# Attention, two feed-forward layers: output stores moved in the last stage, its last block taken product by product, and another order of the opening

## The chip, the core and the metric

The kernel runs on one core of one Trainium2 chip. The metric is the device time of one execution, in microseconds (us). The engines are named as in the profile: PE (TensorE; PEld is its weight load), DVE (VectorE), ACT (ScalarE), POOL (GpSimd) and SP (SyncE, which here issues the DMAs).

## The reference

Three layers follow each other on 3072 tokens of 512 values (4 batches of 768, 8 heads of 64).

- Attention in chunks of 32 queries: each chunk sees 16 keys ahead of it, its own 32, 8 behind it, and 8 memory keys; softmax of the scaled scores, times the values.
- A feed-forward layer with SoLU: `h = x @ w_in` (512 to 1024), `solu = h * softmax(h)`, a layer norm over the 1024 with the gain `g_ln`, and `@ w_out` (1024 to 512).
- A feed-forward layer with hard swish: `h = x @ w_in` (512 to 2048), `g = h * clip(h + 3, 0, 6) / 6`, and `@ w_out` (2048 to 512).

```python
    h = x @ w_in
    e = np.exp(h - np.max(h, axis=-1, keepdims=True))
    solu = h * e / (np.sum(e, axis=-1, keepdims=True) + 1e-09)
    ln = (solu - mu) / np.sqrt(var + 1e-06) * g_ln
    x = ln @ w_out
    ...
    h = x @ w2_in
    out = (h * np.clip(h + 3.0, 0.0, 6.0) / 6.0) @ w2_out
```

The four weight matrices come as 64-bit floats; the other inputs and the output are 32-bit.

## The kernel before

The order of all work is written out by hand. A list of names is run through from the left; each name issues the instructions of one step on the engines that it uses. Each engine takes its own instructions in the order of the list, so the list is the order of every engine and of SP's queue of DMAs at once. What a step has to wait for is worked out from the tiles that it reads and writes.

**Products in two parts.** A 32-bit operand is split into a high part (rounded, by a copy on ACT) and a low part (the rest, by a subtraction, mostly on DVE). Each product is then three matmuls: high by high, high by low, low by high.

**The opening.** `FIRST` is a list of some 530 entries. It brings the kernel from nothing to its steady loop, which starts with token tile 7 (a tile has 128 tokens). Its entries:

- `load_q`, `load_k`, `load_v`, `load_mem_k`: loads of a tile's q, k, v, and of the memory keys, all on SP. `load_v` has ten DMAs for tiles 0 and 1 (two of them `mem_v`), eight for most others; `load_k` has two. Two tiles share a buffer in turn, so the load of tile i waits for the last reader of tile i - 2. `zero` clears a buffer once.
- `q_p`, `k_p` (two parts a tile), `mem_p`: transposes on PE, `q_e`, `k_e`, `mem_e` their copies out of PSUM (L298 on ACT, L300 on DVE or POOL). `s_p`: scores on PE (L522). `s_max`, `s_sub`, `s_exp`, `s_sum`, `s_norm`: the softmax, on DVE but for `s_exp` (ACT) and `s_norm` where the entry names POOL. `p_p`, `p_e`: the probabilities transposed and copied. `v_p`: times the values (L578). `x_h`, `x_l`: the result split.
- `load_w1:u`, u = 0 to 7: a quarter of one half of `w_in`, 512 KB, 64-bit. `w1_abs`, `w1_hold`, `w1_bits` (three steps), `w1_hi`, `w1_lo` turn it into a 32-bit high and low part. `load_wo`, `wo_abs`, ..., `wo_lo` do the same for the first `w_out`, `load_w2`, `w2_abs`, ..., `w2_store` for the second layer's weights.
- `m1:i,f,half`: the first product of tile i (L609). Unit u of `w_in` is f = u // 4 and kt = u % 4; `half` takes kt 0 and 1 or 2 and 3, six matmuls of 512 columns. `m1:0,1,0` needs units 4 and 5, `m1:0,0,0` units 0 and 1.
- `ln_...`: SoLU and layer norm of a tile; `ln_p`, `ln_h`, `ln_l` transpose and split it. `m2:0,n`: the second product of three tiles (L694).
- `warm:n`: n transposes of the identity on PE (L1043), whose results nobody reads.
- An entry's last letter is its engine: A for ACT, D for DVE, P for POOL.

**The loop.** `BODY` is run for tiles 7 to 23. Its first PE step is `m1:0`.

**The last layer** is taken block by block with a scheme of seven products (1 to 7) for each pair of 2 x 2 blocks in place of eight. Its second product runs in `G_SEQ`, 96 units (t, j): t is one of 12 blocks of 256 tokens, j one of 8 pieces of the inner dimension. `g4(i)` (L990) does unit i on PE: seven products of three matmuls with 256 columns, in `ORDER_B`, summed up over j in four PSUM banks (product 1 in bank 0; 6 and 2 in bank 1; 7 and 5 in bank 2; 4 and 3 in bank 3). For odd t, banks 0 and 1 are halves of one tile, and banks 2 and 3 are tiles of their own.

Ahead of `g4(i)`, `g_load` fetches the operand from DRAM (L963, SP), `g_sum` adds and subtracts (L969, DVE), `g_hi` (ACT) and `g_lo` (DVE, both L79x) split it. The loop at the end of the function fetches unit i + 5, prepares i + 3 and the low part of i + 2 in step i. After the last piece of a block (j = 7) its four banks become the output: `q1` (ACT, L998) copies product 1, four `q_sum` (DVE, L1001) add the rest, `q_store` (SP, L1018) issues four stores of 128 KB. Before, this stood in two steps behind the block:

```python
            if j == NU - 1:
                drains = [[("q1", t), ("q_sum", t, 1), ("q_sum", t, 2)],
                          [("q_sum", t, 3), ("q_sum", t, 4), ("q_store", t, 0), ("q_store", t, 1)]]
```

Of the kernel before, what the change touches and what calls it, by code (L numbers as in the profile page):

```python
# [30 lines left out]
    s_max:0 k_p:2,0 k_p:2,1 w1_hold:2,D s_sub:0 s_exp:0 k_e:1,1,A s_p:1 s_sum:0 load_w1:0 w1_abs:0,A w1_bits:2,0
    w1_bits:2,1 s_max:1 k_e:2,1,A load_q:2 load_mem_k:1 k_e:2,0,A w1_hi:3,P q_p:2 s_norm:0,D warm:9 p_p:0 load_w1:4
    w1_bits:2,2 load_k:3 s_sub:1 q_e:2,0,A w1_hold:0,P w1_abs:4,A load_k:4 q_e:2,1,A warm:5 k_p:3,0 w1_hold:4,D
    w1_bits:0,0 p_e:0,1,A w1_bits:0,1 s_p:2 s_exp:1 s_sum:1 mem_p:2 p_e:0,0,A s_norm:1,D w1_bits:4,0 consts load_q:3
# [11 lines left out]
    wo_hold:0,P wo_hold:1,D load_k:7 ln_max:1 s_p:5 p_e:3,1,A s_edge:5 p_e:3,0,A wo_bits:0,0 s_max:5 s_norm:4,D
    k_p:6,1 m1:2,1,0 k_e:6,1,A load_q:6 q_p:6 load_wo:2 wo_abs:2,A m1:2,0,0 wo_hold:2,P ln_sq:0 ln_var:0 ln_pow:0
    load_v:3 k_mem:6,D s_sub:5 wo_bits:1,0 q_e:6,0,A q_e:6,1,A wo_bits:2,0 wo_bits:2,1 v_p:3 ln_exp:1 p_p:4 ln_den:1
    k_p:6,0 x_h:3,1 ln_norm:0 m1:2,0,1 x_l:3,1 s_exp:5 wo_bits:1,1 ln_solu:1 p_e:4,0,A wo_bits:0,1 ln_mean:1
    wo_bits:0,2 p_e:4,1,A ln_p:0,0 wo_bits:2,2 load_wo:3 wo_abs:3,A m1:2,1,1 wo_hold:3,D wo_bits:1,2 k_e:6,0,A wo_g:0  # L50
    ln_h:0,0,1 ln_sq:1 s_p:6 wo_hi:0,A wo_g:1 ln_var:1 ln_max:2 s_sum:5 s_norm:5,D wo_hi:1,P load_q:7 wo_bits:5,0
    s_edge:6 ln_l:0,0,1 load_v:4 v_p:4 ln_p:0,1 ln_exp:2 ln_pow:1 load_wo:4 m1:3,0,0 wo_abs:4,A load_wo:6 q_p:7
    load_q:8 q_e:7,1,A x_h:4,1 ln_h:0,1,1 m1:3,1,0 load_k:8 m1:3,1,1 x_l:4,1 ln_den:2 k_p:7,1 k_e:7,1,A wo_g:2
    m1:3,0,1 wo_hi:2,A q_e:7,0,A k_p:7,0 ln_norm:1 ln_l:0,1,1 s_max:6 ln_solu:2 ln_mean:2 s_sub:6 p_p:5 ln_sq:2
    ln_p:1,0 wo_lo:0,P ln_max:3 s_exp:6 k_e:7,0,A m1:4,1,0 p_e:5,0,D wo_bits:5,1 ln_var:2 wo_bits:3,0 wo_lo:1,P
    wo_bits:3,1 ln_p:1,1 wo_bits:5,2 load_k:9 wo_abs:6,A m1:4,0,0 ln_exp:3 ln_pow:2 ln_h:1,0,1 m1:4,1,1 ln_den:3
    ln_norm:2 p_e:5,1,A wo_bits:3,2 ln_solu:3 early_close ln_p:2,0 load_v:5 m1:4,0,1 wo_hold:4,P ln_l:1,0,1 wo_g:3
    ln_max:4 load_wo:7 s_sum:6 ln_h:1,1,1 wo_bits:4,0 ln_h:2,0,1 wo_bits:4,1 ln_exp:4 s_p:7 load_q:9 ln_l:1,1,1 v_p:5
    ln_l:2,0,1 ln_mean:3 x_h:5,1 ln_sq:3 wo_hold:6,P load_v:6 ln_den:4 ln_p:2,1 ln_h:2,1,1 ln_solu:4 ln_mean:4 k_p:8,0
    m2:0,0 wo_hi:3,D q_p:8 q_e:8,1,A x_l:5,1 ln_var:3 ln_pow:3 q_e:8,0,A m2:0,3 ln_sq:4 wo_bits:6,0 wo_bits:6,1  # L60
    k_p:8,1 m1:5,0 s_norm:6,P s_max:7 k_e:8,0,D s_sub:7 wo_bits:6,2 ln_var:4 wo_g:5 s_exp:7 k_e:8,1,A p_p:6 p_e:6,1,A
    wo_bits:4,2 wo_g:4 load_v:7 wo_lo:2,P wo_lo:3,D ln_norm:3 m1:5,1 wo_hi:5,P s_sum:7 p_e:6,0,A wo_hi:4,A wo_lo:4,P
    v_p:6 s_p:8 ln_max:5 ln_exp:5 ln_p:3,1 x_h:6,1 ln_l:2,1,1 m2:0,1 ln_p:3,0 ln_h:3,0,1 ln_h:3,1,0 wo_abs:7,D wo_g:6
    load_w2:1 wo_hi:6,A wo_hold:7,D s_norm:7,P ln_den:5 m2:0,4 ln_solu:5 wo_bits:7,0 wo_bits:7,1 p_p:7 wo_bits:7,2
    p_e:7,1,A x_l:6,1 m1:6,1 m1:6,0 ln_mean:5 p_e:7,0,D wo_g:7 wo_lo:6,D load_w2:0 ln_l:3,1,0 v_p:7 wo_lo:5,D load_v:9
    wo_hi:7,P ln_sq:5 ln_var:5 ln_pow:4 w2_abs:1,A ln_norm:4 ln_pow:5 ln_p:4,1 ln_max:6 wo_lo:7,P ln_exp:6 m2:0,2
    load_k:10 m2_e:0,0 ln_p:4,0 w2_abs:0,A ln_den:6 s_max:8 w2_hold:1,D m2:0,5 w2_bits:1,0 w2_bits:1,1 w2_bits:1,2
    load_w2:3 w2_store:1 ln_l:3,0,1 m2_e:0,1 m2:0,6 m2:0,7 m2:0,9 m2_s:0,1 ln_h:4,1,0 x_h:7,0 m2:0,10 x_l:7,0
    ln_solu:6 ln_mean:6 ln_norm:5 ln_sq:6 ln_p:5,1 m2:0,11 ln_p:5,0 ln_l:4,1,0 ln_h:5,1,0 ln_h:4,0,0 w2_abs:3,A
    m2_s:0,0 ln_l:5,1,0 m2:0,8 ln_l:4,0,0 ln_var:6 ln_pow:6 w2_hold:3,P ln_norm:6 m2_e:0,3 m2_e:0,2 load_v:8 s_sub:8  # L70
# [1292 lines left out]
```

## Time and profile before

| What | Value |
|---|---|
| Time, median of 3 runs | 877.47 us (877.0 to 877.73) |
| The profiled execution, its own time | 878.19 us |
| Its span, first to last instruction | 876.4 us |
| PE busy | 859.8 us, 98% of the span |
| DVE busy | 749.3 us, 86% |
| ACT busy | 466.8 us, 53% |
| POOL busy | 263.9 us, 30% |

All times in the rows count from the start of the span. A busy PE in the table counts the whole length of each matmul, and matmuls overlap; waits are what a matmul stood idle for. The chain of work that ended last is 80% PE and 9% DVE.

### The profile page before, as it was taken

The page shows a single profiled execution, that of the slowest core. Times are in us where ns is not written, and L with a number is a line of the kernel's source. Part 1 is how long each engine was busy: PE and PEld are TensorE (multiplying, and loading weights), DVE is VectorE, ACT ScalarE, POOL GpSimd, SP SyncE. Part 2 cuts the span into 40 slices and gives each one's busy share as a digit, 9 for nine tenths or more (in the row PEclk, how much of TensorE's full clock was granted, in tenths as well). Part 3 has the DMA queues.
Part 4 walks back from the last instruction along what each step waited for, and adds up shares of the span by engine and source line. Part 5 has one row for each costly group of instructions (what it writes and reads, how often), then busy time and mean ns, then how long its engine had stood idle before and what let it go on. Part 6 is the DMA issues. An engine that isn't in the chain of part 4 may idle for free.

```text
span 876.4 us, 20127 instructions
## 1 busy us (share of the span) xinstructions
PE 859.8 (98%) x7523; PEld 811.8 (93%) x7523; DVE 749.3 (86%) x1593; ACT 466.8 (53%) x865; POOL 263.9 (30%) x233
## 2 busy tenths in 40 slices
...
PEclk9999999999999999999999999999999999999999
...
GB/s 228 190 234 132 86 127 205 255 196 266 272 273 248 234 297 224 149 169 224 249 182 135 240 143 215 185 157 228 255 261 219 169 138 138 147 124 135 136 137 74
DMA packets 184013, 168.26 MB, mean 192 GB/s; under 512 B 107116, under 2 KB 154220, under 8 KB 183916
## 3 DMA queue, kind: packets, MB, share of 16 engines
...
## 4 chain that ended last, share of the span: by engine, by line
PE 80%; DVE 9%; DMA 5%; issue 2%; ACT 2%; SPq 2%; POOL 0%; ACTq 0%; DVEq 0%; POOLq 0%
PE acc L903 25%; PE acc L990 20%; PE m L694 14%; PE h L609 12%; PE tp L666 2%; PE tp L578 2%; PE sc L522 2%; DMA q_raw<-in_q_dram 1%; DVE f_s L1001 1%; PE tp L560 1%; PE tp L509 1%; DVE f_xl L969 1%; DMA w1raw<-in_moe_w_in_dram 1%; DVE f_kn L969 1%; PE tp L494 1%
## 5 line engine op out<-in xcount | busy, mean ns | idle before, releaser
L694 PE MATMUL m<-lnh,wo 128*128 128x384 f32 x512 | 138.3, 344 | 0.0
L938 ACT ACTIVATE f_s<-f_e,constants 128x512 f32<-128x512 f32 x96 | 68.1, 720 | 76.5 <-DVE f_e L931 60.5
L609 PE MATMUL h<-w,xh 128*128 128x512 f32 x336 | 106.3, 397 | 0.1
L694 PEld LDWEIGHTS m<-lnh,wo 128*128 128x128 f32 x512 | 91.7, 189 | 0.2
L694 PE MATMUL m<-lnl,wo 128*128 128x384 f32 x256 | 88.2, 345 | 0.0
L311 POOL TENSOR_SCALAR w2t<-w2t 128x512 f32<-128x512 f32 x30 | 58.9, 1965 | 44.9 <-ACT w2t L304 44.9
L609 PEld LDWEIGHTS h<-w,xh 128*128 128x128 f32 x336 | 61.0, 188 | 11.6 <-ACT lnh L337 0.3
L941 DVE SCALAR_TENSOR_TENSOR f_s<-f_s,f_e 128x512 f32<-128x512 f32 x96 | 70.5, 742 | 0.9 <-ACT f_s L938 0.9
L609 PE MATMUL h<-w,xl 128*128 128x512 f32 x168 | 65.7, 391 | 0.0
L298 ACT ACTIVATE kT<-tp 128x448 f32<-128x448 f32 (+3 forms) x61 | 24.7, 457 | 53.6 <-PE tp L494 46.2
L694 PEld LDWEIGHTS m<-lnl,wo 128*128 128x128 f32 x256 | 48.2, 189 | 0.0
L793 ACT ACTIVATE b_qb<-f_kn 128x384 fp32r<-128x384 f32 (+1 forms) x48 | 27.4, 571 | 33.8 <-DVE f_kn L969 27.6
L624 ACT ACTIVATE e<-h,lst 128x1024 f32<-128x1024 f32 x24 | 26.5, 1103 | 24.1 <-DVE lst L618 24.0
L298 ACT ACTIVATE qb<-tp 64x512 f32<-64x512 f32 x48 | 28.5, 593 | 19.4 <-PE tp L509 18.9
L609 PEld LDWEIGHTS h<-w,xl 128*128 128x128 f32 x168 | 31.5, 188 | 6.9
L935 DVE TENSOR_TENSOR f_e<-acc,f_e 128x512 f32<-128x512 f32 x48 | 32.9, 685 | 2.1 <-PE acc L903 0.4
L793 ACT ACTIVATE b_km<-f_xl 128x512 fp32r<-128x512 f32 x26 | 16.4, 631 | 34.2 <-DVE f_xl L969 26.6
L927 DVE TENSOR_TENSOR f_e<-acc,f_e 128x512 f32<-128x512 f32 x48 | 32.8, 684 | 1.2 <-PE acc L903 0.3
L341 DVE TENSOR_TENSOR lnl<-tp,lnh 128x512 fp32r<-128x512 f32 x41 | 26.7, 686 | 7.7 <-ACT lnh L337 7.7
L618 DVE TENSOR_REDUCE lst<-h 128x1 f32<-128x1024 f32 x24 | 29.2, 1217 | 4.4 <-PE h L609 4.2
L644 ACT ACTIVATE e<-so,lst 128x1024 f32<-128x1024 f32 x24 | 27.4, 1143 | 7.6 <-DVE lst L640 7.6
L635 DVE SCALAR_TENSOR_TENSOR so<-h,lst,e 128x1024 f32<-128x1024 f32 x24 | 30.7, 1278 | 0.5
...
## 6 DMA issues: line engine op xcount, KB each, us to landing
...
```

The costliest lines, as they stand in the source:

```text
L298: ACT.activation(out=out, in_=in_, func=AF.Copy)
L311: ENG[eng].tensor_scalar(out=tf, in0=tf, scalar1=U_LO, scalar2=U_HI, op0=ALU.max, op1=ALU.min)
L609: PE.matmul(h[:, f], a[:, kt], w[kt][:, f * 512:(f + 1) * 512], start=n == 0, stop=n == 3 * NKT - 1)
L635: DVE.scalar_tensor_tensor(out=so_t[i], in0=h_t.pop(i).rearrange("p a b -> p (a b)"), scalar=st[:, 5:6], in1=e_t[i], op0=ALU.mult, op1=ALU ...
L694: PE.matmul(acc, w[fc // 2][:, fc % 2, dc * P:(dc + 1) * P], a[:, fc], start=n == 0, stop=n == len(todo) - 1)
L793: ACT.activation(out=hl[0], in_=r, func=AF.Copy)
L903: PE.matmul(o, w[wl][:, c * P:(c + 1) * P], x[xl][:, c], start=m == 0 and half == 0, stop=m == 5, skip_group_check=True)
L927: DVE.tensor_tensor(c_of(n)[1], bank(n % 2, 2), wide(c_of(n)[0][:, 1]), ALU.add)
L935: DVE.tensor_tensor(c, bank(n % 2, 3), c, ALU.add)
L938: ACT.activation(out=g_of(n)[k], in_=c_of(n)[k], func=AF.Relu, bias=three, scale=1.0)
L941: DVE.scalar_tensor_tensor(out=g_of(n)[k], in0=g_of(n)[k], scalar=6.0, in1=c_of(n)[k], op0=ALU.min, op1=ALU.mult)
L990: PE.matmul(bank(t % 2, k)[:, half], g[al][:, G_BLOCK[p]], b_op[j, p][bl], start=j == 0 and m == 0 and half == 0, stop=j == NU - 1 and m = ...
```

## The change

Three things change.

**Stores of a block.** The sums and stores behind a block stand in four steps of the loop instead of two: `q1` and the first sum; the second; the third and fourth; the stores.

**The last block.** The last two units (t = 11, j = 6 and 7) are no longer taken one after the other. Products 1, 6 and 2 of both come first, then 7 and 5 of both, then 4 of both, then 3 of both. Then come `q1` and the sums; the fourth sum is taken in two halves (`q_half`), and each of the four stores is issued behind its data, two of them by ACT.

**The opening.** `FIRST` has the same steps in another order. 61 warm transposes stand for 71. The engine of some entries changes: 19 entries that named DVE no longer do, 24 others now do; POOL loses 14 and gains 9, ACT loses and gains 14.

```diff
 FIRST = """
-    zero:v1,P load_q:0 zero:qb,P zero:pb,P load_w1:1 zero:v0,D warm:15 q_p:0 zero:km0,D load_mem_k:0 zero:kn1,D
-    zero:kn0,P w1_abs:1,D warm:12 mem_p:0 w1_hold:1,P mem_e:0,D load_w1:3 zero:km1,D w1_abs:3,D load_k:0 q_e:0,1,A
...
-    q_p:3 s_max:2 k_e:3,0,A mem_p:1 q_e:3,0,A w1_bits:0,2 mem_e:2,A q_e:3,1,A s_sub:2 load_v:0 spread_mem_v:0,0,A
-    load_q:4 warm:4 k_p:3,1 mem_e:1,D w1_lo:3,D k_e:3,1,A s_exp:2 k_p:4,1 s_p:3 load_w1:6 w1_hi:0,P
-    spread_mem_v:0,64,A warm:1 v_p:0 s_sum:2 k_e:4,1,A p_p:1 load_w1:5 w1_hi:2,A x_h:0,0 w1_bits:4,1 w1_abs:6,A
-    k_p:4,0 load_v:1 w1_lo:2,D p_e:1,1,A load_k:5 warm:1 q_p:4 p_e:1,0,A load_w1:7 x_l:0,0 w1_hold:6,D w1_bits:6,0
-    w1_abs:5,D w1_lo:0,P s_max:3 k_e:4,0,A w1_bits:4,2 load_q:5 s_norm:2,P m1:0,0,0 q_e:4,1,A s_sub:3 w1_bits:6,1
-    w1_bits:6,2 w1_hold:5,P p_p:2 load_k:6 w1_bits:5,0 spread_mem_v:1,64,A m1:0,0,1 spread_mem_v:1,0,A v_p:1 q_e:4,0,A
-    w1_hi:6,A w1_bits:5,1 s_p:4 k_p:5,1 x_h:1,0 w1_hi:4,A x_l:1,0 early_open m1:1,0,0 w1_bits:5,2 p_e:2,0,A p_e:2,1,A
-    w1_abs:7,A s_max:4 load_wo:5 w1_hi:5,A w1_hold:7,D q_p:5 w1_lo:6,P k_p:5,0 load_wo:0 q_e:5,0,A w1_lo:5,D
...
+    zero:kn0,P zero:km0,D zero:kn1,D load_w1:4 zero:km1,D zero:v0,D w1_abs:4,D w1_hold:4,D w1_bits:4,0 zero:pb,P
+    w1_bits:4,1 w1_bits:4,2 zero:v1,P load_mem_k:0 warm:20 mem_p:0 mem_e:0,A load_mem_k:3 load_k:0 load_q:0 load_w1:0
+    warm:3 k_p:0,0 w1_hi:4,D k_e:0,0,A q_p:0 zero:qb,P q_e:0,1,A k_p:0,1 mem_p:3 q_e:0,0,A k_mem:0,D mem_e:3,D
...
+    load_k:3 mem_p:1 q_e:2,0,A s_sub:1 load_q:3 k_p:2,1 k_e:2,1,A w1_bits:6,2 mem_e:1,A w1_bits:7,2 w1_bits:5,0
+    k_p:3,1 k_p:3,0 load_v:0 s_exp:1 load_k:4 w1_hi:7,A w1_bits:5,1 s_sum:1 spread_mem_v:0,64,A load_w1:1 s_p:2
+    s_norm:1,P spread_mem_v:0,0,A q_p:3 load_q:4 k_e:3,1,A warm:2 v_p:0 w1_lo:7,D k_e:3,0,A q_e:3,1,A s_max:2 k_p:4,1
+    q_e:3,0,D w1_bits:5,2 w1_hi:6,A w1_lo:6,P w1_hi:5,A w1_lo:5,P s_sub:2 x_h:0,0 x_l:0,0 load_w1:3 s_exp:2 p_p:1
+    p_e:1,0,A w1_abs:1,A p_e:1,1,A s_p:3 k_p:4,0 k_e:4,0,A k_e:4,1,A m1:0,1,0 s_sum:2 s_norm:2,D q_p:4 p_p:2 load_v:1
+    w1_hold:1,P load_w1:2 s_max:3 s_sub:3 q_e:4,1,A m1:0,1,1 w1_bits:1,0 w1_abs:3,D w1_bits:1,1 w1_bits:1,2 w1_hi:1,D
+    load_k:5 w1_lo:1,D q_e:4,0,A spread_mem_v:1,0,A s_p:4 spread_mem_v:1,64,A v_p:1 x_h:1,0 load_q:5 w1_hold:3,P
+    w1_bits:3,0 p_e:2,0,A w1_bits:3,1 consts w1_abs:2,A x_l:1,0 w1_bits:3,2 w1_hold:2,D load_v:2 load_wo:7 p_e:2,1,A
+    m1:0,0,0 w1_bits:2,0 w1_bits:2,1 early_open m1:1,0,0 w1_bits:2,2 w1_hi:3,A w1_hi:2,A w1_lo:2,P load_k:6 s_exp:3
+    w1_lo:3,D k_p:5,1 k_e:5,1,D q_p:5 q_e:5,0,A k_p:5,0 k_e:5,0,A q_e:5,1,A s_max:4 load_g s_sum:3 s_norm:3,D m1:1,1,0
...
+    wo_hold:3,D wo_g:5 ln_mean:4 ln_h:2,1,1 load_wo:6 wo_lo:0,D ln_solu:3 early_close ln_sq:4 ln_mean:3 wo_hi:1,A
+    m1:5,0 k_e:8,0,A wo_g:2 ln_sq:3 wo_hi:2,A p_p:6 m1:5,1 wo_bits:3,0 load_q:8 wo_g:4 wo_bits:3,1 wo_lo:1,D ln_var:3
+    ln_l:2,1,1 wo_bits:3,2 m2:0,0 ln_var:4 wo_hi:5,A ln_pow:3 ln_pow:4 p_e:6,0,A wo_hi:4,A wo_lo:4,P wo_g:3 p_e:6,1,A
...
-    def g4(i):
+    def g4(i, products=ORDER_B):
         t, j = G_SEQ[i]
         g = g_hl(i)
-        for p in ORDER_B:
+        for p in products:
...
+    def q_half(t, n):
+        c = out_of(t)[1][:, n]
+        sixth(c, bank(t % 2, 3)[:, n], c)
+
+    def q_put(t, k, n, eng=SP):
+        h = 1 - n if k == 0 else n
+        eng.dma_start(out=out[t * TG + n * P:t * TG + (n + 1) * P, 256 * h:256 * h + 256], in_=out_of(t)[k][:, n])
...
-            if i > 23:
+            if 23 < i < len(G_SEQ) - 2:
                 emit("g4", i)
...
             if j == NU - 1:
-                drains = [[("q1", t), ("q_sum", t, 1), ("q_sum", t, 2)],
-                          [("q_sum", t, 3), ("q_sum", t, 4), ("q_store", t, 0), ("q_store", t, 1)]]
-        for step in drains:
-            for name, *a in step:
-                emit(name, *a)
+                drains = [[("q1", t), ("q_sum", t, 1)], [("q_sum", t, 2)], [("q_sum", t, 3), ("q_sum", t, 4)],
+                          [("q_store", t, 0), ("q_store", t, 1)]]
+        for products in ((1, 6, 2), (7, 5), (4,), (3,)):
+            for i in (len(G_SEQ) - 2, len(G_SEQ) - 1):
+                g4(i, products)
+        q1(t)
+        q_sum(t, 1)
+        q_put(t, 0, 1, ACT)
+        q_sum(t, 2)
+        q_sum(t, 3)
+        q_put(t, 0, 0, ACT)
+        q_half(t, 0)
+        q_put(t, 1, 0)
+        q_half(t, 1)
+        q_put(t, 1, 1)
```

## Rows read from the trace of the kernel before

**Rows 1.** The page: span, and PE's granted clock (tenths) in 40 slices.
```profile
span 876.4 us, 20127 instructions
...
PEclk9999999999999999999999999999999999999999
```

**Rows 2.** Busy times by stretch: PE, PEld, DVE, ACT, POOL; clock, DMA share, GB/s.
```profile
48.00:92.00 44.00, 41.63 (x398) 32.91 (x396) 41.08 (x84) 34.42 (x61) 25.43 (x19) 1.00 0.68 162
...
675.00:871.00 196.00, 194.26 (x1688) 192.48 (x1687) 177.74 (x512) 86.36 (x168) 0.00 (x0) 1.00 0.42 132
```

**Rows 3.** Waits of PE from 32 to 92 us: total, times, longest (eight rows, four shown).
```profile
PE tp L509 <- DMA q_raw<-in_q_dram: 1.6, 1, 1.6
PE tp L666 <- ACT lnh L337: 1.0, 1, 1.0
...
PE tp L560 <- ACT pb L298: 0.4, 1, 0.4
...
PE tp L480 <- DMA kn<-in_k_dram: 0.2, 1, 0.2
```

**Rows 4.** Waits of PE from 675 to 871 us.
```profile
PE acc L990 <- DVE b_v L796: 0.8, 2, 0.6
PE acc L990 <- DVE b_kT L796: 0.7, 4, 0.2
```

**Rows 5.** Timeline of the tail, all engines: start, length, instructions, idle time ahead.
```profile
865.92 2.20 PE L990 MATMUL acc<-b_ll,b_v 128*128 128x256 f32 x18
...
866.60 0.68 DVE L796 TENSOR_TENSOR b_e<-f_kn,b_e 128x512 fp32r<-128x512 f32 x1
...
868.30 2.20 PE L990 MATMUL acc<-b_wo,b_e 128*128 128x256 f32 x18
869.52 0.38 ACT L998 ACTIVATE f_pe<-acc 128x256 f32<-128x256 f32 x1 [3.16 <-PE acc L990]
...
870.34 0.50 PE L990 MATMUL acc<-b_pn,b_e 128*128 128x256 f32 x3
870.73 1.95 DVE L1001 SCALAR_TENSOR_TENSOR f_s<-acc,f_s 128x512 f32<-128x512 f32 x3
871.91 1.80 SPq L1018 DMA_DIRECT2D out_dram<-f_s  x4
```

**Rows 6.** The output sums' line L1001: shortest, median and longest in ns.
```profile
L1001 DVE SCALAR_TENSOR_TENSOR f_s<-acc,f_s x36: 411/691/692, 675.0 to 872.0; 128x512 f32<-128x512 f32 x24, 128x256 f32<-128x256 f32 x12
```

**Rows 7.** Timeline of SP's queue behind a block's end, 733 to 765 us.
```profile
740.70 1.80 SPq L1018 DMA_DIRECT2D out_dram<-f_s  x4
742.61 0.53 SPq L963 DMA_DIRECT2D f_z<-g  x1
```

**Rows 8.** Waits of DVE from 675 to 872 us.
```profile
DVE f_kn L969 <- DMA f_z<-g: 8.0, 9, 2.2
```

**Rows 9.** Groups by line and form, 0 to 110 us: a low part on DVE.
```profile
L384 DVE TENSOR_TENSOR w<-w1raw,w 128x512 fp32r<-128x512 f32 x4 | 2.8, 690 | 0.3 <-ACT w L298 0.2
```

**Rows 10.** Timeline of PE in the opening.
```profile
1.34 3.46 PE L1043 MATMUL idle<-ident 128*128 128x128 f32 x15 [1.34 <-POOL ident masks.py:199]
...
5.39 1.47 PE L1043 MATMUL idle<-ident 128*128 128x128 f32 x12
...
28.74 1.17 PE L578 MATMUL tp<-pb,v 128*64 128x64 f32 x32
...
31.95 0.70 PE L609 MATMUL h<-w,xh 128*128 128x512 f32 x2
...
39.70 1.64 PE L609 MATMUL h<-w,xx 128*128 128x512 f32 x6
42.98 0.63 PE L509 MATMUL tp<-ident,q_raw 128*128 128x128 f32 x4 [1.64 <-DMA q_raw<-in_q_dram]
```

**Rows 11.** Timeline of SP's queue in the opening.
```profile
23.89 2.48 SPq L273 DMA_DIRECT2D v<-in_v_dram  x4
...
37.27 0.43 SPq L239 DMA_DIRECT2D q_raw<-in_q_dram  x1
```

More of the change, by code (lines that the diff above doesn't have):

```diff
@@ L31 @@
[L31 to L34, printed above, removed]
-    q_p:3 s_max:2 k_e:3,0,A mem_p:1 q_e:3,0,A w1_bits:0,2 mem_e:2,A q_e:3,1,A s_sub:2 load_v:0 spread_mem_v:0,0,A
@@ L46 @@
[L46 to L70, printed above, removed]
@@ new lines @@
+    s_max:0 s_sub:0 s_exp:0 s_sum:0 load_w1:5 load_q:1 warm:16 q_p:1 q_e:1,1,A s_norm:0,D w1_hi:0,P k_p:1,0 warm:13
+    p_p:0 k_e:1,0,A w1_lo:0,P load_w1:7 q_e:1,0,A k_e:1,1,A s_p:1 w1_lo:4,P w1_abs:7,D w1_hold:7,D w1_bits:7,0
+    load_w1:6 p_e:0,1,A w1_abs:6,A w1_bits:7,1 load_mem_k:2 w1_hold:6,D load_mem_k:1 mem_p:2 load_k:2 w1_bits:6,0
+    p_e:0,0,A mem_e:2,A s_max:1 w1_bits:6,1 warm:3 k_p:2,0 load_q:2 w1_abs:5,A k_e:2,0,A w1_hold:5,P q_p:2 q_e:2,1,A
+    load_k:3 mem_p:1 q_e:2,0,A s_sub:1 load_q:3 k_p:2,1 k_e:2,1,A w1_bits:6,2 mem_e:1,A w1_bits:7,2 w1_bits:5,0
@@ new lines @@
+    wo_abs:4,A wo_hold:7,D x_h:2,0 k_p:6,1 m1:1,0,1 x_l:2,0 k_e:6,1,D load_q:6 load_wo:5 wo_hold:4,D ln_mean:0 p_p:3
+    s_norm:4,P p_e:3,0,A m1:1,1,1 ln_max:1 q_p:6 ln_sq:0 wo_bits:7,0 ln_var:0 ln_pow:0 q_e:6,0,A wo_abs:5,D k_mem:6,D
+    m1:2,0,0 q_e:6,1,A wo_hold:5,P k_p:6,0 load_wo:0 wo_bits:4,0 s_max:5 m1:2,1,0 ln_exp:1 wo_abs:0,D k_e:6,0,A
+    m1:2,1,1 p_e:3,1,A wo_bits:4,1 wo_hold:0,P load_v:3 v_p:3 x_h:3,1 ln_den:1 x_l:3,1 p_p:4 load_wo:1 ln_norm:0
+    ln_p:0,0 m1:2,0,1 wo_bits:4,2 p_e:4,0,A p_e:4,1,A wo_bits:5,0 load_v:4 wo_abs:1,A s_sub:5 s_p:6 s_exp:5
@@ new lines @@
+    wo_bits:7,1 wo_bits:7,2 ln_h:0,0,1 ln_solu:1 v_p:4 x_h:4,1 ln_mean:1 wo_hold:1,D ln_p:0,1 wo_bits:5,1 ln_l:0,0,1
+    s_edge:6 ln_max:2 s_sum:5 x_l:4,1 s_norm:5,P load_k:7 k_p:7,0 ln_exp:2 m1:3,1,0 k_e:7,0,D ln_den:2 ln_h:0,1,1
+    ln_l:0,1,1 ln_sq:1 s_max:6 ln_solu:2 load_k:8 k_p:7,1 ln_var:1 ln_pow:1 load_wo:2 wo_abs:2,A wo_bits:1,0 m1:3,0,0
+    wo_bits:1,1 wo_bits:0,0 p_p:5 load_q:7 p_e:5,1,A m1:4,1,0 ln_mean:2 wo_bits:1,2 load_wo:3 ln_sq:2 ln_norm:1
+    load_v:5 m1:4,0,0 s_sub:6 ln_p:1,0 k_e:7,1,A q_p:7 wo_abs:3,A wo_hold:2,P wo_g:7 ln_var:2 wo_g:1 m1:4,0,1
```

26 lines of the change are left out of this document (17 added, 9 removed).

## Prediction

> **What bounds the kernel now.** Read first the span beside the profiled execution's time: 876.4 us of 878.19 lie between first and last instruction, so 1.8 us lie around them [rows 1]. The busy times by stretch then name the bound: PE has 41.63 of 44 us from 48 to 92 us and 194.26 of 196 from 675 us on [rows 2]. Where PE is the bound, only three things can shorten the kernel: PE's waits, what PE does before its work can start, and what is left when PE stops. So the second view is that of PE's waits, by stretch. From 32 to 92 us PE waits 4.8 us in eight places, the longest 1.6, the others 0.2 to 1.0 [rows 3]. In the last product's stage, from 675 us, it waits 1.5 us in six places, always for a low part that DVE makes [rows 4]. The reader should see that little is to be had: 4.8 us in the opening, 1.5 us in the blocks, and the tail. The third view is the timeline of the tail: PE's last matmul ends at 870.34 + 0.50 = 870.84 us and the span at 876.4, so 5.56 us follow PE [rows 5].
>
> A shift of PE's opening is kept to the end: from the loop on, all that PE waits for is derived from what PE has made, and no clock time is fixed.
>
> **The tail, by terms.** Before: `q1` starts only at 869.52, after nine matmuls of the last unit (products 1, 6, 2, which share a tile), then the four sums run on DVE, the last three in 1.95 us from 870.73 to 872.68 [rows 5]. That is 1.84 us after PE. Four stores are issued from 871.91 in 1.80 us, to 873.71, 0.45 each, and the last lands 2.69 us later, at the span's end [rows 5].
>
> After: the last two units run product by product. Their 42 matmuls take what they take now, 870.84 - 865.92 = 4.92 us, 0.117 each [rows 5]. Eighteen of them end the first two banks at 868.0, and `q1` (0.38) and the first sum (0.69) follow by 869.2. Thirty end the third bank at 869.4, so sums 2 and 3 (0.69 and 0.41 [rows 6]) are done by 870.6. Behind PE's end are two halves of 0.41 instead of 1.84. Taken with 0.1 for the wait, the last half is done at 870.84 + 0.1 + 0.82 = 871.76, its store is issued by 872.2 and lands at 874.9: **1.5 us less**. If the first half is released by product 4 alone, it is 1.9; if each step adds what stands between the sums now (about 0.1), 1.1. I take 1.5, because `q1` waited for a whole tile and not for its own half.
>
> The two stores on ACT leave its queue at 869.2 and 870.6, when ACT has nothing else. They save SP two issues of 0.45, already in the sum above, where SP issues one store ahead of the last. The Trainium skill ("DMA: Bandwidth & Descriptors", section "Issuing engines are not separate DMA queues") says that all issuers share the same 16 DMA engines and that a second one saves only sequencer time. By that rule no transfer gets shorter, and the sum stays at 1.5; whoever counted two queues as twice the bandwidth would book about 0.3 us more.
>
> The new order asks for the last unit's operands earlier: its first product starts nine matmuls after 865.92, at 866.97, not at 868.30. Its low part is whole at 866.60 + 0.68 = 867.28, and the first matmul that needs the late part of it (third of product 6) comes at 866.97 + 5 x 0.117 = 867.55 [rows 5]. Free by 0.27 us; if that margin is gone it costs at most 0.3.
>
> **The blocks' stores.** Now all sums and stores of a block stand in two steps of the loop. SP reaches `q_store` and waits for DVE's last sums: at 740.70 it issues four stores in 1.80 us, and only then, at 742.61, the next `g_load` [rows 7]. That load is late by the wait and by the issues, and DVE then waits for it: 8.0 us in nine places, 0.9 a block [rows 8]. DVE is busy 177.74 of 196 us there [rows 2], so it recovers slowly, and PE's 1.5 us of waits follow. After: sums in three steps, stores in a fourth, when their data is there. SP's 1.80 us then lie in a step in which the next load would wait for DVE anyway (one unit is 21 x 0.117 = 2.46 us of PE). Gain between 0 (the waits have another source) and 1.5 (all). I take **1.2 us**, near the upper end, since each wait is for DVE and DVE gets back 8 us.
>
> **The opening.** The list has the same steps but for ten warm transposes fewer (61 for 71), another order, and other engines for some: DVE loses 19 entries and gains 24. Net five at no more than 0.69 [rows 9] is 0 to 3.4 us; by their kinds I take 2.3. It is hidden while DVE is not the bound: from 48 to 92 us it is busy 41.08 of 44 [rows 2].
>
> First the way to the first real product. `m1` starts at 31.95, 3.2 us after `v_p:0` at 28.74, and that needs the ten loads of `load_v:0`, the last of them issued by 23.89 + 2.48 = 26.37 [rows 10, 11]. Ahead of them the new order has the same four q, four k and five weight loads, without `load_k:4`, which now follows. Some 300 KB less, about 1 us, which `load_k:4` gives back, since `k_p:4` stands between `v_p:0` and the first `m1`. Start of `m1`: 31 to 32.5, no gain taken. The ten warm transposes (0.12 each [rows 10]) lie in that wait and bring nothing.
>
> Then `q_p:5`: PE stops at 41.34 and goes on at 42.98, when q5 lands, issued at 37.27 [rows 10, 11]. Ahead of `load_q:5` both orders have the same loads, so it lands at about the same time. But PE now does four halves of `m1` before `q_p:5`, not three. The fourth takes about 1.4 us (six matmuls from 39.70 to 41.34, less the drain [rows 10]) and fills the wait: **1.4 us**. It needs weight unit 1, loaded after `load_k:4`; its conversion ends near 37 us by these durations, about when PE gets there. Bounds: a gain of all 4.8 us [rows 3], a loss as in the rivals.
>
> **Sum.** 1.5 + 1.2 + 1.4 = 4.1 us: the profiled execution would go from 878.19 to 874.1. That execution is 0.72 above the median of the runs, 877.47, so the median would be **873.4**, 0.47% faster. A measurement tells apart about 0.2%, 1.75 us.
>
> **Rivals.**
> *Opening freed.* With products later in the list (`m2:0,0` stands behind both halves of `m1:5`), the other waits of 32 to 92 us vanish too, 4.8 for 1.4: 877.47 - 1.5 - 1.2 - 4.8 = 870.0. For it: DVE has more time until each is due. Against it: a new order makes new waits. 0.15.
>
> *DVE takes it back.* The 2.3 us fall where DVE is full: opening -1.4 + 2.3 = +0.9, in all 875.7. The change then does what it says only in the tail and blocks. For it: 41.08 of 44. Against: its work on `w_out` and on tiles 0 to 2 is due later, since the first `m2` moves behind 5.7 us of `m1` (the halves of `m1:5`). 0.16.
>
> *`load_k:4` too late.* It is issued behind ten v loads, near 26.4. If it needs as long as q5 did (37.27 to 42.98), it lands near 32.9, (26.4 + 5.7 and 0.8 for its other issue), and the first `m1` comes 3.2 us behind it, as it now comes behind `v_p:0`: 36.1. From there to `q_p:5` PE needs 9.4 us now (31.95 to 41.34), less 1.0 of waits in it (two of 0.4, one of 0.2 [rows 3]), plus 1.4 for a half of `m1` and 0.4 for `q_p:4`, so 10.2. It gets there at 46.3, 3.3 late, less the 1.4 done ahead: +1.9 in the opening, -0.8 in all, 876.7. Against: the queue is emptier behind the small v loads. 0.14.
>
> *Slower: PE falls to its lower clock.* The first fifteen transposes take 3.46 us, 0.23 each, the next twelve 1.47, 0.12 each [rows 10]: half the rate and the full one, though the granted clock reads 9 tenths or more throughout [rows 1]. The new list has two warm transposes (0.23 us) ahead of `v_p:0` and nothing else to do until v0 lands, a gap of perhaps 3 us (by the durations its list is through near 25.5; v0 was used at 28.74). If PE ran at 1.2 GHz from there to `q_p:5`, its 12 us of work would double: +12 - 1.6 - 1.4 = +9 in the opening, 883.8 in all. It decides from 5.9 us of doubled work on (4.1 + 1.75). Against it: behind the 1.64 us gap four transposes take 0.63 at 42.98, where 0.23 each would make 0.92 [rows 10]. The Trainium skill ("TensorE: Matmul & The Clock Gate", "What's actually happening") calls the slow state the default that activity lifts, so fewer fillers speak for this rival; no row shows a fall. 0.09.
>
> **Chances and range.** The forecast, 871.9 to 875.3, has 0.46. Faster by over 0.2%: 0.46 + 0.15 + 0.10 of the DVE rival (its 875.7 lies on the bound) = 0.71; within: 0.06 + 0.14 = 0.20; slower: 0.09. The range 869.6 to 878.6 reaches from the freed opening to past the late load, and leaves out the slow clock and some 0.05 at the lower end.
>
> **What would show it.** Tail: the last DVE sum ends under 1.1 us after PE, and the span 4.0 to 4.2 us after PE. Blocks: no `q_store` between a late `g_load` and its fellows, DVE's wait for `f_z` far under 8.0 us, PE's waits from 675 us under 0.5. Opening: first `m1` at 31 to 32.5, the wait ahead of `q_p:5` shorter or gone, the loop's first `m1` at about 123 for 124.46. Wrong it would be if the loop starts later than 126, or if new waits on loads stand in PE's list there.

## The result and the profile after

The changed kernel takes 868.53 us (median of 4 runs, 867.68 to 870.68) against 877.6 (4 runs, 877.0 to 881.25) of the kernel before beside it: a ratio of 0.9891, 95% interval 0.9869 to 0.9912. It is 8.9 us below the 877.47 of the prediction, which had forecast 4.1 of them and ended its range at 869.6.

The profiled execution took 867.68 us. Its span is 10.5 us shorter than that of [rows 1]. The page after, span and granted clock:

```profile
span 865.9 us, 20130 instructions
...
PEclk9899999999999999999999999999999999999999
```

The busy times by stretch after (columns as in [rows 2]):

```profile
23.00:29.00 6.00, 6.00 (x59) 4.72 (x60) 4.12 (x9) 4.75 (x8) 1.22 (x1) 0.50 0.83 208
...
32.00:48.00 16.00, 16.00 (x175) 12.67 (x171) 15.42 (x29) 10.89 (x20) 6.02 (x6) 1.00 0.83 202
48.00:92.00 44.00, 43.54 (x381) 34.92 (x378) 42.82 (x96) 38.15 (x68) 23.80 (x19) 1.00 0.64 157
664.00:861.60 197.60, 197.58 (x1741) 197.20 (x1739) 183.32 (x533) 93.01 (x174) 0.00 (x0) 1.00 0.44 142
```

From 48 to 92 us PE was busy 41.63 us before and is 43.54 now, though DVE has 1.7 us more to do there (42.82 for 41.08). In the last stage PE no longer stops. The new thing is the first row: from 23 to 29 us the clock was granted at half, 1.2 GHz.

The waits of PE from 32 to 92 us, one where [rows 3] had eight with 4.8 us (from 675 to 871 us, [rows 4], none is left):

```profile
PE tp L666 <- DVE so L659: 0.4, 1, 0.4
```

PE's timeline in the opening after, against [rows 10]: values of tile 0, first `m1`, q5, the loop's first `m1`; and the issue of q5 on SP, against [rows 11]:

```profile
28.29 1.56 PE L578 MATMUL tp<-pb,v 128*64 128x64 f32 x32
...
33.15 0.73 PE L609 MATMUL h<-w,xh 128*128 128x512 f32 x2
...
42.68 0.66 PE L509 MATMUL tp<-ident,q_raw 128*128 128x128 f32 x4
...
120.21 0.71 PE L609 MATMUL h<-w,xh 128*128 128x512 f32 x2
```

```profile
35.40 0.38 SPq L239 DMA_DIRECT2D q_raw<-in_q_dram  x1
```

SP's queue behind a block's end after, against [rows 7]: the four stores now stand between loads that are on time. DVE's waits in that stage, against [rows 8]: that for `f_z` is gone, the others are its sums waiting for their copies and for PE.

```profile
733.90 0.52 SPq L963 DMA_DIRECT2D f_xh<-g  x1
735.03 1.78 SPq L1021 DMA_DIRECT2D out_dram<-f_s  x4
736.91 0.52 SPq L963 DMA_DIRECT2D f_kn<-g  x1
```

```profile
DVE f_s L1001 <- ACT f_pe L998: 8.0, 5, 4.7
DVE f_s L1001 <- ACT f_e L998: 4.0, 5, 1.0
DVE f_s L1001 <- PE acc L990: 0.7, 2, 0.5
```

The tail after, against [rows 5]:

```profile
858.89 0.38 ACT L998 ACTIVATE f_pe<-acc 128x256 f32<-128x256 f32 x1 [5.25 <-PE acc L990]
859.31 0.69 DVE L1001 SCALAR_TENSOR_TENSOR f_s<-acc,f_pe 128x512 f32<-128x512 f32 x1 [4.74 <-ACT f_pe L998]
...
860.03 1.74 ACTq L1021 DMA_DIRECT2D out_dram<-f_s  x2
...
861.08 0.50 PE L990 MATMUL acc<-b_pn,b_e 128*128 128x256 f32 x3
861.88 0.76 DVE L1001 SCALAR_TENSOR_TENSOR f_s<-acc,f_s 128x256 f32<-128x256 f32 x2 [0.47 <-PE acc L990]
862.33 1.09 SPq L1021 DMA_DIRECT2D out_dram<-f_s  x2
```

PE ends at 861.08 + 0.50 = 861.58, the sums at 862.64, the span 4.3 us after PE (5.56 before).

The loop's first `m1` in the kernel before, and its one wait near 212 us:

```profile
124.46 0.63 PE L609 MATMUL h<-w,xh 128*128 128x512 f32 x2
```

```profile
PE tp L560 <- POOL pn L552: 0.7, 1, 0.7
```

**Where the 10.5 us came from.** The loop's first `m1` stands at 120.21 for 124.46: **4.25**. From there to PE's end there are 741.4 us for 746.4: **5.0**, of which 0.7 is that wait, which only the profile of before shows, and 4.2 lie in the last stage, from its first matmul on L990 to the last (231.3 us for 235.5). The tail: **1.24**. These are two executions: in further profiles the loop starts at 123.5 to 125.9 us with the old list (e1, e2, e4, e10, e15 below) and at 119.5 to 119.8 with the new one (e3, e9, e12, e16).

### The profile page after: what moved, and what is told of

The parts are those of the page before. It is cut to its first block, busy times and chain, and to the rows that moved or that the text cites. A ratio compares the mean times of both kernels' runs of the same rounds, so it can differ in the third digit from the quotient of the medians.

```text
span 865.9 us, 20130 instructions
## 1 busy us (share of the span) xinstructions
PE 858.0 (99%) x7513; PEld 811.9 (94%) x7513; DVE 747.1 (86%) x1599; ACT 469.7 (54%) x865; POOL 259.3 (30%) x228
## 4 chain that ended last, share of the span: by engine, by line
PE 88%; DVE 6%; ACT 2%; DMA 2%; issue 1%; SPq 0%; DVEq 0%; ACTq 0%
PE acc L903 25%; PE acc L990 24%; PE m L694 15%; PE h L609 12%; PE tp L666 3%; PE sc L522 3%; PE tp L578 2%; PE tp L560 1%; PE tp L509 1%; PE tp L494 1%; DMA w1raw<-in_moe_w_in_dram 1%; DMA b_ll<-b_d 1%; PE tp L480 1%; DMA f_z<-g 1%; ACT e L644 0%
## 5 line engine op out<-in xcount | busy, mean ns | idle before, releaser
L941 DVE SCALAR_TENSOR_TENSOR f_s<-f_s,f_e 128x512 f32<-128x512 f32 x96 | 68.5, 722 | 0.9 <-ACT f_s L938 0.9
L552 POOL TENSOR_TENSOR pn<-pe,ast 128x512 f32<-128x512 f32 x19 | 20.0, 1053 | 45.8 <-DVE ast L548 31.1
L624 ACT ACTIVATE e<-h,lst 128x1024 f32<-128x1024 f32 x24 | 26.4, 1100 | 12.1 <-DVE lst L618 11.9
```

What stands on the lines that cost most here:

```text
L941: DVE.scalar_tensor_tensor(out=g_of(n)[k], in0=g_of(n)[k], scalar=6.0, in1=c_of(n)[k], op0=ALU.min, op1=ALU.mult)
```

## Experiments

Each was timed beside the kernel before on its chip, where that took 876.1 to 878.7 us. "Loop to PE end" is the time from the loop's first `m1` to the end of PE's last matmul, both read from its timeline. Of the kernels made from the one before, the list of the opening is called old; "two steps" are the old sums and stores behind a block (`drains` in the code).

### The parts alone

```diff
 e1 (before, but:)
-                drains = [[("q1", t), ("q_sum", t, 1), ("q_sum", t, 2)],
-                          [("q_sum", t, 3), ("q_sum", t, 4), ("q_store", t, 0), ("q_store", t, 1)]]
+                drains = [[("q1", t), ("q_sum", t, 1)], [("q_sum", t, 2)], [("q_sum", t, 3), ("q_sum", t, 4)],
+                          [("q_store", t, 0), ("q_store", t, 1)]]
 e2 (after, with the old FIRST and the old two steps)
 e3 (before, with the new FIRST)
```

> The kernel before, with only the sums and stores behind a block spread over four steps. Ledger theory (from the trace after: PE runs 4.2 us shorter through the second product of the last layer, while the matmul rows of before showed waits of only 1.5): 4.2 us less than before, near 873.3. Rival, the prediction's size: at most the 1.5 us of waits in PE's matmul rows, near 876.0. In both the profile shows no PE wait from 675 us on and DVE's wait for f_z under 1 us.

> The kernel before, with only the last two units taken product by product and the last stores issued behind their data. Theory: 1.2 us less (the span ends 4.3 us after PE's last matmul, for 5.6 before), near 876.2, and PE itself no longer than before. Rival: PE waits for the last unit's low part, asked for 1.3 us earlier, and half of it is lost: near 876.9.

> The kernel before, with only the new order of the opening. Ledger theory: the loop starts 4.2 us earlier (120.2 for 124.5), and the wait of the loop near 212 us is gone too (0.75): 5.0 us less, near 872.5. Rival, the prediction's size: only the wait for q5 is filled, 1.4 us less, near 876. The granted clock falls to 0.5 between 22 and 30 us as in the kernel after.

Blocks alone: 873.27 us, ratio 0.9958 (0.9938 to 0.9977), 3.0 us less than the kernel before beside it, where 4.2 had been expected; 742.0 us from the loop to PE's end, and no wait of PE from 675 us. Last block alone: 874.99, 0.9984 (0.9964 to 1.0003), an interval that includes no change; its span ends 4.84 us after PE, not 4.3. Opening alone: 869.34, 0.9925 (0.9901 to 0.995), a larger gain than either forecast.

Together the ratios would give 1.33% where the whole change gives 1.09%; the intervals are too wide to tell these two apart. That the parts overlap shows in the trace of e3: its loop begins at 119.62, and although the blocks' steps are the old ones, PE needs only 742.3 us from the loop to its end and waits nowhere from 675 us.

### Order or engines

```diff
 e5 (after: the new order, each entry with its old engine), e.g.
-k_p:5,1 k_e:5,1,D q_p:5
+k_p:5,1 k_e:5,1,A q_p:5
 e6 (after: the old order, each entry with its new engine)
```

> The changed kernel, but each entry of the new list keeps the engine that it named in the old list. Theory (the gain of the opening is one of order: products stand where PE used to wait): the loop's first m1 starts within 1 us of the 120.2 us of the changed kernel, and the time is 868 to 870.5 us. Rival (other engines for the copies and conversions make it): the loop starts near 123 to 124.5 us, and the time is 871.5 to 873.5 us.

> The changed kernel, but the list of the opening in its old order, each entry with its new engine. Theory (order): the opening gains nothing or loses some, since DVE has five entries more: the loop starts at 123.5 to 126 us, the time is 871.5 to 875 us. Rival (engines): the loop starts at 120 to 122 us, the time is 868 to 870.5 us.

Both theories fall. 881.27 us, ratio 1.0055 (1.0034 to 1.0075), loop at 134.56; and 886.32, 1.0117 (1.0094 to 1.014), loop at 139.33. Either half alone costs the opening 10 to 15 us. The largest waits of PE in e5 and in e6, 32 to 140 us (the list takes one line there, so line numbers are 45 lower):

```profile
PE sc L477 <- ACT qb L253: 2.7, 1, 2.7
PE tp L435 <- ACT far L290: 1.4, 2, 1.2
PE sc L477 <- DVE pe L494: 1.3, 1, 1.3
```

```profile
PE tp L515 <- DVE lst L584: 4.0, 1, 4.0
PE tp L621 <- DVE so L614: 1.7, 2, 1.2
PE tp L515 <- ACT v L253: 1.5, 1, 1.5
```

All these waits end with a step of ACT or DVE: copies, softmax, layer norm. They are not the whole loss. The granted clock has a mean of 0.95 from the start to the loop in both, where the kernel before has 1.00 and the changed one 0.97; no run tells how the loss divides between waits and clock. The order is only good for the engines that it was laid out for.

### One wait at a time

```diff
 e7 (after)
-m1:0,0,0 w1_bits:2,0 ... k_e:5,1,D q_p:5 q_e:5,0,A
+w1_bits:2,0 ... k_e:5,1,D q_p:5 m1:0,0,0 q_e:5,0,A
 e13 (before)
-p_e:1,1,A load_k:5 ... w1_bits:4,2 load_q:5 s_norm:2,P
+p_e:1,1,A load_q:5 load_k:5 ... w1_bits:4,2 s_norm:2,P
 e14 (e13, and)
-ln_sq:1 s_p:6 ... s_edge:6 ln_l:0,0,1 load_v:4 v_p:4
+ln_sq:1 ... ln_l:0,0,1 load_v:4 v_p:4 s_p:6 s_edge:6
```

> The changed kernel with one entry moved: the half of m1 that stands ahead of the transposes of q5 stands behind them. The prediction's term (this half fills 1.4 us of the wait for q5): q5's transposes wait 1 to 1.6 us for their load, the loop starts 1 to 1.6 us later than 120.2, the time is 1 to 1.6 us longer than that of the changed kernel. Rival (q5 has landed by then in any case, because its load is issued some 2 us sooner): no wait above 0.3 us, loop and time within 0.5 us of the changed kernel.

> The kernel before with one entry of the old list moved: the load of q5 is issued ahead of the fifth tile's keys and of weight unit 7. Theory (the opening's length is PE's work and its waits in a row, so a wait that goes is a gain): no wait for q5 above 0.4 us, the loop's first m1 1.2 to 1.9 us sooner than 124.5 to 125.9 us (the two executions of the old list), the time 1 to 2 us below the kernel before. Rival (the work behind it is late as well, on DVE above all, and PE only waits further on): the wait for q5 goes, others grow by as much, loop and time within 0.5 us.

> As the last one, and the scores of tile 6 stand behind the product with the values of tile 4 in place of ahead of it (their copy of the keys was 0.8 us late). Theory (waits add up): another 0.5 to 0.8 us, 1.6 to 2.7 us below the kernel before. Rival (the list's order fits its copies and loads, and a move makes new waits): the wait of 0.8 us is replaced by one for the values of tile 4 or by a later one, no gain over the last one, or a loss.

e7: 867.61 us, loop at 119.76; q5's transposes start at 40.84 without a wait, with one half of `m1` less ahead of them (and, ahead of them, a new wait of 0.7 for the operand of the next half, less than the 1.4 that the half takes). So the fourth half is not what filled q5's wait; q5 is there sooner, its load issued at 34.28. e13: 876.64 us, ratio 0.9996 (0.9977 to 1.0016). The wait for q5 is gone from 32 to 92 us, and two others stand in its place:

```profile
PE tp L578 <- DMA v<-in_v_dram: 1.8, 1, 1.8
PE tp L480 <- DMA kn<-in_k_dram: 1.1, 1, 1.1
```

The keys do not land later than before. PE comes to them sooner, at 37.43 us for 38.69, and goes on with them at 38.55 for 38.88. A wait for values at that place (tile 3) is there in e10 too, 0.8 us, with nothing moved. So a wait that is taken away lets PE run into the next load. e14: 875.59, 0.999 (0.9973 to 1.0007), the loop at 123.20: its two targets are gone, waits for values of 1.8 us in two places remain. A microsecond at most, and not certain. What e13 and e14 show is that the old list's waits can't be taken off one by one at their length.

### The clock

```diff
 e8 (after)
-s_max:1 w1_bits:6,1 warm:3 k_p:2,0 ... load_k:3 mem_p:1 q_e:2,0,A
+s_max:1 w1_bits:6,1 warm:11 k_p:2,0 ... load_k:3 mem_p:1 warm:6 q_e:2,0,A
 e11 (e7 and e8 together)
```

> The changed kernel with 14 more warm transposes (11 for 3 ahead of the second tile's keys, 6 behind the second part of the memory's keys). Theory (the granted clock falls between 22 and 30 us because PE does only thin work ahead of it, and that costs about 3 us): the clock stays at 0.95 or more from 20 to 30 us, the scores that took 1.97 us take about 1.15, the 14 transposes cost 0 to 1.6 us and the loop starts 1 to 3 us sooner than at 120.2: 866 to 868.5 us. Rival (loads set the time of v_p:0 and of the first m1, whatever the clock): loop within 0.7 us of 120.2 or later, 868 to 870 us. Rival (the clock does not depend on the thin work): the fall stays in the profile.

> The changed kernel with the 14 more warm transposes and with the half of m1 behind q5. Theory (each takes a little off and they touch other stretches): 866 to 867.3 us, loop's first m1 at 118.8 to 119.4 us. Rival (the loop's start is set by DVE's work between 48 and 110 us, not by what PE does ahead of 35 us): within 0.5 us of the changed kernel's 867.6 to 868.5 us, loop at 119.4 to 120.2 us.

e8: 867.45 us, loop at 119.39. From 23 to 29 us its clock is at the full level:

```profile
23.00:29.00 6.00, 5.62 (x84) 4.38 (x84) 4.03 (x8) 5.39 (x10) 1.66 (x2) 1.00 0.78 195
```

With the slow clock PE fills the 6 us; with the full one it works 5.62 and waits. The fall lies where PE has time to spare, and removing it gives nothing that is measured (867.59 for the changed kernel once more, below). e11: 868.17, loop at 121.42. The time lies where the rival put it, the loop later than in both forecasts: no gain either.

### Sums or stores

```diff
 e4 (before)
+                drains = [[("q1", t), ("q_sum", t, 1), ("q_sum", t, 2)], [("q_sum", t, 3), ("q_sum", t, 4)],
+                          [("q_store", t, 0), ("q_store", t, 1)]]
 e15 (before)
+                drains = [[("q1", t), ("q_sum", t, 1)], [("q_sum", t, 2)],
+                          [("q_sum", t, 3), ("q_sum", t, 4), ("q_store", t, 0), ("q_store", t, 1)]]
 e9 (after, with the old two steps); e10 (before, unchanged)
```

> The kernel before, with the sums in two steps as before and only the stores moved to a third step. If PE's stalls come from the operand load that stands behind the stores in SP's queue (the prediction), this alone brings nearly all that the four steps bring: about 4 us less, DVE's wait for f_z under 1 us for 8.0. Rival: the stalls come from 1.4 us of sums in one step of DVE, which pushes the low parts out: then 0 to 1.5 us less, and PE's waits for b_kT stay.

> The kernel before, with the sums of a block spread over three steps of the loop as in the change, but the stores still in the step of the last two sums. Theory (stores that SP issues ahead of the next load are what makes DVE wait, and DVE waits longer where that issue takes longer than 1.8 us): DVE's wait for the loaded operand stays, 4 to 8 us, in another step; time within 1.5 us of the kernel before. Rival (the pile of sums on DVE is the cause): DVE's wait goes below 1.5 us and the time is 2.5 to 3.7 us below the kernel before, as with the stores moved alone.

> The changed kernel with the sums and stores of a block in two steps of the loop, as before. Theory (with the new opening the waits in the blocks are gone already, as where only the opening was new): PE needs 741 to 743 us from the loop's start to its last matmul, at most 1 us of waits from 675 us, and the time is 868 to 870 us, 0 to 1.5 us above the changed kernel. Rival (the two parts add up as each is worth alone): 2.5 to 3.7 us of waits come back, PE needs 744 us or more, the time is 871 to 872.5 us.

> The kernel before, once more, for a second look at its waits. Theory (the waits in the blocks differ from execution to execution, since the loads that they hang on have no fixed margin): PE's waits from 675 us and DVE's for the loaded operand differ from 1.5 and 8.0 us by more than a third, and the time from the loop's start to PE's end is 742 to 745.5 us. Rival (they are the same in each execution of the old order): 1.2 to 1.8 and 7 to 9 us, 746 us or more.

e4: 873.01 us, ratio 0.9958 (0.9938 to 0.9978), 3.2 us less than the kernel before, 741.0 us from loop to PE end, and DVE's wait for `f_z` down to 1.0: the late load was behind the stores, as the prediction said. But e15, with the stores left ahead of a load, is as fast: 872.08, 0.9951 (0.993 to 0.9972), 742.4 us. DVE still waits there, for another load:

```profile
DVE f_xl L969 <- DMA f_xh<-g: 5.9, 8, 1.6
```

So the theory has the wait right and its price wrong, and the rival the time right and the wait wrong: DVE's wait alone doesn't stop PE. It does so on top of two sums in one step; taking either away is enough. e10 (one run, 878.55 us): 745.3 us, at the upper edge of the 742 to 745.5 forecast, with PE's waits at 1.0 and `f_z` at 6.9. PE's waits differ by a third from the first profile, DVE's by less, so that forecast is half right; the waits are of the old order, not of one draw. e9: 868.31, 0.9907 (0.9883 to 0.993), 742.4 us. With the new opening the four steps are worth some 1 us on PE and nothing that is measured.

### What the opening has to do with the last stage

With two steps and the old opening, five executions need 744.0 to 746.4 us from loop to PE end (before, e2, e10, e13, e14), with the new one 742.3 and 742.4. The stores differ. SP issues the four of a block in 1.80 us as a rule, but some take up to 3.46, and the load behind them is late by as much. In e10:

```profile
722.11 2.73 SPq L1018 DMA_DIRECT2D out_dram<-f_s  x4
...
780.56 3.36 SPq L1018 DMA_DIRECT2D out_dram<-f_s  x4
```

The view of the DMA queues, asked in windows of half a microsecond, has one packet of the queue named "instruction" starting within each of these two issues. All issues of four stores that take over 2.5 us in the kernels with two steps (and the two of e15) stand so, but for one of 2.53 in e10 (at 690.12), where the packet is of 8 KB and of a second queue with that name. Those of e9, none of which meets such a packet, take 1.8 (2.0 for one). Its first block's stores are issued in pairs, and the first pair does meet one and takes 2.32 for 1.07. The queue moves 59 packets in a run, 0.97 MB, 16.4 KB each; PE's 15,026 matmuls and weight loads, divided by 59, are 255 a packet. If they are PE's, a few more instructions on PE must shift them against the stores:

```diff
 e17 (before)
-warm:20 k_p:0,0
+warm:42 k_p:0,0
 e18 (e9)
-warm:20 mem_p:0
+warm:46 mem_p:0
```

> The kernel before with 22 more warm transposes (42 for 20 ahead of the first tile's keys), and nothing else. They put 44 more instructions into PE's stream, so each packet of instructions for PE would come 44 instructions sooner in the last stage, 2.5 us at 42 instructions in 2.39 us. Theory (a store's issue is stretched where such a packet occupies one of the DMA engines, and that is what makes PE wait in the blocks): no store 596 and 655 us behind the loop's first m1 takes over 2.0 us to issue, DVE waits 5.5 us or less for the loaded operand, and PE needs 742 to 743.5 us from the loop's start to its end, where the five executions with the old opening and the old two steps need 744.0 to 746.4. What the warm transposes cost in the opening (0 to 2.6 us) stands apart. Rival (the packets have nothing to do with it): stretched stores at the same places, 744 to 746.4 us.

> The changed kernel with the old two steps behind a block (as measured before), and 26 more warm transposes (46 for 20 ahead of the memory's keys): 52 more instructions for PE, 3.0 us in the last stage, so that the packets that start near 718.1 and 778 us come at about 715 and 775 us of the old count, while SP issues the stores of a block. Theory: one or two of these stores take 2.5 to 3.5 us to issue in place of 1.8, DVE waits 5.5 to 8 us for the loaded operand in place of 4.7, and PE needs 743 to 746 us from the loop's start to its end in place of 742.4. Rival: no stretched store there, 742 to 742.7 us.

e18: 872.32 us, ratio 0.9937 (0.9921 to 0.9953), 745.0 us from loop to PE end, `f_z` 7.3 us. Stores of e9 and then of e18, the same block:

```profile
773.54 1.80 SPq L1021 DMA_DIRECT2D out_dram<-f_s  x4
```

```profile
773.84 3.01 SPq L1021 DMA_DIRECT2D out_dram<-f_s  x4
...
833.40 2.89 SPq L1021 DMA_DIRECT2D out_dram<-f_s  x4
```

The DMA queues of e18 from 773.8 to 777.8 us (second line: GB/s in 40 slices of 0.1 us):

```profile
GB/s 0 0 0 0 0 0 0 164 72 246 358 307 195 123 287 328 338 195 10 0 0 10 0 10 10 10 10 10 20 31 92 266 358 369 205 144 328 348 328 215
...
q8 instruction: 1, 0.02, 2.2%
```

The slices ahead of the gap add up to two stores (0.26 MB), then for 1.1 us there is hardly anything but a thread of 10 GB/s, then come the other two. In e9 there is no such packet and no such gap between the stores.

e17: 879.66 us, ratio 1.0013 (0.9996 to 1.003). The two stores that were stretched take 1.80 now (at 725.12 and 782.70), as the theory says, but its 742 to 743.5 us didn't come: 747.35. The packets, 2.5 to 4.1 us sooner against the stores, now meet two others, and PE waits 1.4 us more near 640 us, ahead of the first block's end, for low parts of DVE:

```profile
692.85 3.48 SPq L1018 DMA_DIRECT2D out_dram<-f_s  x4
...
840.98 3.06 SPq L1018 DMA_DIRECT2D out_dram<-f_s  x4
```

Packets start within these, at 693.9 and 841.7. That packets and stretched stores move together is shown; how a packet holds up SP's issue isn't. Nor does any run show what moved the packets between the old list and the new one, which has ten warm transposes fewer.

### Who issues the last stores; the change once more

```diff
 e12 (after)
-        q_put(t, 0, 1, ACT)
+        q_put(t, 0, 1)
-        q_put(t, 0, 0, ACT)
+        q_put(t, 0, 0)
 e16 (after, unchanged)
```

> The changed kernel with all four stores of the last block issued by SP. Theory (a second issuing engine saves only issue time, and the last store is ahead of its transfer's 2.3 to 2.7 us either way): the span ends 4.2 to 4.8 us behind PE's last matmul, the time is within 0.5 us of the changed kernel. Rival (SP's issues stand one behind the other and push the last by two of 0.45 us): the span ends 5.1 to 5.3 us behind PE, the time is 0.8 to 1 us longer.

> The changed kernel once more. Theory (the opening's and the blocks' gains belong to the order and are there in each execution): the loop's first m1 at 119.6 to 120.6 us, 741 to 742 us from there to PE's last matmul, the granted clock falls again between 20 and 30 us, time 867 to 869.5 us. Rival (part of it was the draw of the one profile): the loop a microsecond or more off 120.2, or 743 us and more to PE's end.

e12: 867.07 us, ratio 0.9893 (0.9871 to 0.9916), the span 4.3 us after PE as with ACT. The two early stores are out before the last halves are there, whoever issues them. e16: 867.59, 0.9905 (0.9881 to 0.9929), loop at 119.48 (0.1 sooner than forecast), 741.2 us to PE's end, the clock 0.83 from 20 to 30 us where the first profile has 0.66. Gain and fall of the clock are there again; the first `m1` is not where it was (31.13 us for 33.15).

## Why the prediction was wrong

Two terms of the sum failed: the opening (1.4 forecast, 4.25 measured at the loop's start) and the blocks (1.2 forecast, 4.2 measured in the last stage). So did a sentence that both rest on, "a shift of PE's opening is kept to the end": with only the opening new (e3), PE needs 742.3 us behind the loop's start, where the kernels with the old opening and the old two steps need 744.0 to 746.4.

**Tail: right.** 1.24 us for 1.5 (1.1 to 1.9). The last sum ends 1.06 us after PE, under the 1.1 forecast; the two halves go together behind PE's last product, so the first is not early. ACT's part brings nothing (e12), as the Trainium skill's rule on issuing engines ("DMA: Bandwidth & Descriptors", "Issuing engines are not separate DMA queues") had it. The profiles of the changed kernel's near relations (e7, e8, e9, e11, e12, e16, e18) also end 4.2 to 4.3 us after PE; with the same tail e5 and e6 end 3.8 after it, and e2 4.84, its last store landing 3.5 us behind its issue for 2.4.

**Blocks: mechanism half right, the term mis-sized.** "Gain between 0 and 1.5 (all)" took PE's matmul rows for the whole loss. The last stage lost 4.2 us more before than after. Matmuls overlap in the rows (0.28 us each, 0.115 apart), so a stop must outlast the overlap to show. PEld's rows in the kernel before, from 675 to 871 us, show the same stops at twice the length of [rows 4]:

```profile
PEld acc L990 <- DVE b_kT L796: 1.8, 5, 0.4
PEld acc L990 <- DVE b_v L796: 1.2, 2, 0.8
```

They are not further waits. The longest stop stands in both:

```profile
787.09 0.62 PE L990 MATMUL acc<-b_ll,b_v 128*128 128x256 f32 x3 [0.64 <-DVE b_v L796]
787.09 0.41 PEld L990 LDWEIGHTS acc<-b_ll,b_v 128*128 128x128 f32 x3 [0.84 <-DVE b_v L796]
```

Taken from start to start of the matmuls, where the undisturbed step is 0.113 us, the stops from 675 us add up to 4.0 us.

Alone the part is worth 3.0 (e1). The load behind the stores is the source of DVE's wait, but the pile of sums is as much part of PE's (e15), and the missing cause is the stretched stores (e18); with the new opening they are gone even where the two steps stay (e3, e9).

**Opening: the wrong case was taken.** The step "the fourth half fills the wait: 1.4 us" falls: without that half PE doesn't wait for q5 either (e7). Its premise, that q5 "lands at about the same time", is what was wrong: the load is issued at 35.40 for 37.27 (at 34.28 in e7, where PE goes on with q5 at 40.84 for 42.98). What happened is the rival "Opening freed", given 0.15: of 4.8 us of waits 0.4 are left (1.1 in e16), and from the first `m1` to the loop there are 87.06 us for 92.51, 5.4 less. The reason that the rival gave, that DVE has more time until each step is due, was not tested: which moves took away the waits other than q5's stays open. Its price of 870.0 was the best of the four, and too high by what the blocks gave. Against it stood "a new order makes new waits". That holds for lists with parts exchanged (e5, e6, e13), not for this one.

**First `m1`.** 33.15, not 31 to 32.5: 1.2 later than before. This is of that one execution: it stands at 31.13 in e16, the same kernel, at 32.06 without the fall of the clock (e8), and at 31.2 to 33.2 with the old list untouched (e1, e4).

**The other rivals.** DVE got its load (1.7 us more from 48 to 92 us, 2.3 forecast), and PE didn't wait for it. `load_k:4` was issued at 22.76, not near 26.4, and PE has no wait for it. The clock did fall, but from 22 us and not in a gap ahead of `v_p:0`, and with no loss that e8 could get back: the 12 us of doubled work were priced as if PE had nothing to wait for in them. What half the clock costs where PE is late already no run shows by itself; in e6 PE runs at half from 116 to 122 us, behind the wait of 4.0.
